# Column halves for the last expert's second weight alone, eight split output rows, and zero products before the last left half

## Chip, cores, metric

One core of one Trainium2 chip. The metric is the device time of one execution in microseconds (us); lower is better. The span of the trace is some 1.8 us shorter than that time. Most of what follows happens in the last 25 us of about 157.

## The reference

Attention with a per-head mask feeds a soft mixture of experts. Only its last part matters here:

```python
for e in range(E):                                   # 8 experts, 4 slots each
    h = np.maximum(slot_input[e] @ w1[e], 0.0)
    slot_out[e] = h @ w2[e]                          # w2[e]: 1024 x 512, float32
slot_out = slot_out.reshape(n_slots, D)
c = softmax(logits, axis=1)                          # 3072 x 32
return (c @ slot_out).astype(np.float32)             # 3072 x 512, 6 MB
```

Every output row needs the slots of all eight experts, so no row is final before the last w2 has landed. A column of the output needs only that column of each w2.

## The kernel before

The weights are loaded from float32 in HBM to bf16 in SBUF by GpSimd's DMA queue, one load after the other; w2 of experts 5, 6 and 7 comes last. It comes in column halves, all left halves first, so that the left columns of some output rows can be computed and stored while the right halves still load. In this document 5L is the left half of expert 5's w2, 7R the right half of expert 7's, and so on. A "row" r is one of 24 groups of 128 output rows (256 KB); a left or right half row has 128 KB.

```python
    def w_half(e, cs):
        nc.gpsimd.dma_start(w2s[e][:, :, cs], w2v[e][:, :, cs])
    # ... (cut)
    w_half(5, left)
    # ... w_half(6, left), w_half(7, left) (cut)
    for e in (5, 6, 7):
        w_half(e, right)
    # ... attention's end, expert products of the first layer, experts 0 to 4 (cut)
    for e in (5, 6, 7):
        second(e, (0,), spread=True)          # 8 products of 256 columns each: left half
    NL = 12                                   # rows that are split
    # product(): one matmul to a PSUM bank, evicted and scaled by DVE (even r) or ACT (odd r)
    V.tensor_copy(slot_out[:, left], sp[0])
    half_rows(left, 0, (2, 2, 4, 4), (1, 2), nc.gpsimd)      # left halves of rows 0 to 11, 4 stores
    for e in (5, 6, 7):
        second(e, (1,), spread=True)          # right half
    V.tensor_copy(slot_out[:, right], sp[1])
    # rows 12 to 23 whole: groups of 1, 1, 2, 4, 4 rows, stored by nc.sync (cut)
    half_rows(right, 2, (4, 4, 4), (1, 2), nc.sync)          # right halves of rows 0 to 11
```

The softmax here doesn't subtract the row's maximum and nothing guards it: scores larger than these inputs give would overflow.

Of the kernel before, what the change touches and what calls it, by code (L numbers as in the profile page):

```python
# [10 lines left out]
F32 = mybir.dt.float32  # L11
# [27 lines left out]
def kernel(  # L39
# [13 lines left out]
    nc = tc.nc  # L53
    P = 128
# [3 lines left out]
    NE, DM, F = moe_w1.shape  # L58
# [16 lines left out]
    def single(shape, dt, name, tag=None):  # L75
        return singles.tile(shape, dt, name=name, tag=tag or name)

    w1s = [single([P, 4, F], BF16, f"w1_{e}") for e in range(NE)]
    w2s = [single([P, 8, DM], BF16, f"w2_{e}") for e in range(NE - 3)] + [None] * 3
# [45 lines left out]
    w2v = [moe_w2[e].rearrange("(fi fo) d -> fi fo d", fo=8) for e in range(NE)]  # L125
# [80 lines left out]
    def x_transpose(n, i0=0, i1=6):  # L206
        b, hp = n // 4, n % 4
        tp = trp.tile([P, S], BF16, tag="tr", name="tpx")
        for i in range(i0, i1):
            nc.tensor.transpose(tp[:, i * 128:(i + 1) * 128], xb[b][:, i, hp * 128:(hp + 1) * 128], ident)  # L210
        nc.vector.tensor_copy(xT[:, hp, i0 * 128:i1 * 128], tp[:, i0 * 128:i1 * 128])  # L211
# [51 lines left out]
    def keep_busy(t, count):  # L263
        for _ in range(count):
            nc.tensor.matmul(t, zero[:, :P], zero, start=True, stop=True)

    idle = pvp.tile([P, 512], F32, tag="pv", name="idle")
# [52 lines left out]
    for n in range(NP):  # L320
# [12 lines left out]
        b, r = n // 4 - 1, n % 4  # L333
# [62 lines left out]
    left, right, full = slice(0, 256), slice(256, 512), slice(0, 512)  # L396

    def w_half(e, cs):
        nc.gpsimd.dma_start(w2s[e][:, :, cs], w2v[e][:, :, cs])  # L399

    w2s[5] = single([P, 8, DM], BF16, "w2_5", tag="msk")
    w_half(5, left)
    w2s[6] = ptp.tile([P, 8, DM], BF16, tag="pT", name="w2_6")
    w_half(6, left)


    def bank(t, shape=(P, 512), dt=F32):
        pool, tag = ((scp, "sc"), (trp, "tr"), (pvp, "pv"))[t]
        return pool.tile(list(shape), dt, tag=tag, name="bank")
# [28 lines left out]
    logits_mm(bl, (0, 1, 2))  # L438
    w2s[7] = ptp.tile([P, 8, DM], BF16, tag="pT", name="w2_7")
    w_half(7, left)  # L440
    for e in (5, 6, 7):
        w_half(e, right)
    x_transpose(last, 0, 3)
    x_transpose(last, 3, 6)
    copies(2, 0)
    idle = bank(2)
# [11 lines left out]
    idle = bank(2)  # L458
# [10 lines left out]
    cs = bank(1, (P, 1))  # L469
# [5 lines left out]
    for e4 in range(2):  # L475
        t = xp.tile([P, 2, 512], BF16, tag="xb", name="hs")
# [29 lines left out]
    idle = spt[1][:, 1]  # L506

    def second(e, xs=(0, 1), spread=False):
        e4, g = e // 4, e % 4
        for fo in range(8):  # L510
            c = fo % 4 if spread else g
            for x in xs:
                nc.tensor.matmul(sp[x][32 * c:32 * c + 32, :], hT[e4][:, fo, 32 * g:32 * g + 32],  # L513
                                 w2s[e][:, fo, 256 * x:256 * x + 256],
                                 start=(e4 == 0 and fo == 0), stop=(e == 7 and fo >= 4))
# [11 lines left out]
    for r in range(24):  # L527
        e = expR.rearrange("c (p r) -> c r p", r=24)[:, r]
        er.append(e)
        nc.tensor.matmul(rp[:, r:r + 1], e[:ES], ones[:ES], start=True, stop=True)  # L530
    V.reciprocal(rrow, rp)
    for e in (5, 6, 7):
        second(e, (0,), spread=True)


    NL = 12
    ov = out.rearrange("(p r) d -> p r d", r=24)

    def product(r, o, cs, t):
        op = bank(t, (P, cs.stop - cs.start))  # L540
        nc.tensor.matmul(op, er[r], slot_out[:, cs], start=True, stop=True)  # L541
        if r % 2:
            nc.scalar.activation(o, op, ACT.Copy, scale=rrow[:, r:r + 1])  # L543
        else:
            V.tensor_scalar(o, op, rrow[:, r:r + 1], None, op0=ALU.mult)  # L545

    def half_rows(cs, t0, groups, banks, eng):
        ots = [single([P, n, 256], F32, f"oh{t0 + x}", tag=f"w1_{t0 + x}") for x, n in enumerate((8, NL - 8))]
        r = 0
        for rows in groups:  # L550
            for _ in range(rows):
                product(r, ots[r // 8][:, r % 8], cs, banks[r % len(banks)])
                r += 1
            eng.dma_start(ov[:, r - rows:r, cs], ots[(r - 1) // 8][:, (r - rows) % 8:(r - 1) % 8 + 1])

    V.tensor_copy(slot_out[:, left], sp[0])  # L556
    half_rows(left, 0, (2, 2, 4, 4), (1, 2), nc.gpsimd)
    for e in (5, 6, 7):
        second(e, (1,), spread=True)
    V.tensor_copy(slot_out[:, right], sp[1])  # L560
    r = NL
    for t, groups in enumerate(((1, 1, 2), (4,), (4,))):
        ot, base = single([P, 4, DM], F32, f"ot{t}", tag=f"w1_{4 + t}"), r
        for rows in groups:
            for _ in range(rows):
                product(r, ot[:, r - base], full, (1, 2)[r % 2])
                r += 1
            nc.sync.dma_start(ov[:, r - rows:r, :], ot[:, r - rows - base:r - base])
    half_rows(right, 2, (4, 4, 4), (1, 2), nc.sync)


# [33 lines left out]
```

## Time and profile before

| kernel before | |
|---|---|
| time, median of 6 runs | 157.33 us (156.19 to 157.59) |
| span of the trace | 155.7 us |
| last load (7R) lands | 137.82 us |
| first full-row store issued | 140.40 us |
| last packet of output ends | 154.04 us |

All rows but the first come from the trace; its clock starts at the first instruction. The prediction below shows the lines. "DMA" is the busy share of the core's 16 DMA engines in tenths and "GB/s" what they moved, in 40 equal slices. PE is the engine of the matrix products (PEld loads its weights), DVE and ACT evict and scale results, and GpSimd (POOL) and SP issue DMAs here. The granted clock of PE is 1.00 at full speed and 0.50 at half; "zero products" below are matmuls of zeros whose only use is to keep PE busy. One more line, from the DMA issues (output and input, queue, count, KB each, median us from issue to landing), serves as a yardstick for stores:

```profile
out_dram<-ot SPq DMA_DIRECT2D x2, 256.0 KB, 2.2
```

These are the first two full-row stores. They land 2.2 us after their issue.

### The profile page before, as it was taken

Reading aid. Unit: us, or ns where it says so; the run is one execution under the profiler, and the core shown is the slowest. Engines: PE = TensorE matmul, PEld = TensorE weight load, DVE = VectorE, ACT = ScalarE, POOL = GpSimd, SP = SyncE. Lnnn points to the kernel's source line nnn. Section 1 sums busy time; section 2 is a strip of 40 time slices with the busy share of each in tenths; the row PEclk is TensorE's granted clock in tenths of the full one; section 3 lists DMA queues with packets and bytes.
Section 4 is the critical chain, followed back from the end, with each engine's and each line's share of the span. In section 5 each row is a group of like instructions: output and inputs, shape, how many; then the busy total and the mean of one; then the engine's idle time right before and its main releaser. Section 6 shows DMA issues by size and latency. Waiting matters only on the chain. (4 is left out here: it accounts for less than half of the span.)

```text
span 155.7 us, 5051 instructions
## 1 busy us (share of the span) xinstructions
PE 118.2 (76%) x2239; PEld 74.6 (48%) x2239; DVE 106.8 (69%) x247; ACT 109.8 (71%) x148; POOL 41.1 (26%) x57
## 2 busy tenths in 40 slices
PE   6756598878697979977979979778987897449500
PEld 2324365555465645755656556555633476214300
DVE  2896269999987869978769979678735414429700
ACT  3286489979799998999898999999451512408700
POOL 7673043720350260170084200000480000700000
PEclk9975559999999999999999999999999999956975
DMA  3999999999999999999999999999999999977995
GB/s 54 155 184 203 172 218 203 196 187 189 212 219 202 188 216 198 186 222 195 186 219 200 185 211 223 213 217 215 210 223 190 199 196 199 240 290 283 404 355 183
DMA packets 40535, 32.85 MB, mean 211 GB/s; under 512 B 26050, under 2 KB 37826, under 8 KB 38594
## 3 DMA queue, kind: packets, MB, share of 16 engines
q0 software_dynamic: 38208, 27.82, 115.1%
q1 hardware_dynamic: 2306, 4.72, 8.1%
q8 instruction: 17, 0.28, 0.7%
q14 instruction: 4, 0.03, 0.1%
HBM read 52.49 MB, written 6.29 MB: 377 GB/s over the span
## 5 line engine op out<-in xcount | busy, mean ns | idle before, releaser
L172 ACT ACTIVATE pT<-sc 128x1024 bf16<-128x1024 f32 (+1 forms) x96 | 83.4, 923 | 9.3 <-PE sc L167 8.8
L167 PE MATMUL sc<-Tq,Tk 64*128 64x256 bf16 (+3 forms) x320 | 36.5, 292 | 13.6 <-ACT Tk L151 10.0
L193 PEld LDWEIGHTS <-pT 128*128 128x128 bf16 x672 | 24.9, 99 | 12.2 <-issue 8.0
L184 DVE TENSOR_TENSOR pT<-pT,msk 128x1024 bf16<-128x1024 bf16 (+1 forms) x48 | 29.3, 639 | 0.2 <-ACT pT L172 0.2
L193 PE MATMUL pv<-vb,pT 128*128 128x65 bf16 x352 | 27.5, 196 | 0.3 <-DVE xb L202 0.3
L193 PE MATMUL pv<-vf,pT 128*128 128x65 bf16 x320 | 25.3, 197 | 0.0
L167 PEld LDWEIGHTS <-Tk 64*128 64x128 bf16 x320 | 11.2, 95 | 22.6 <-ACT Tk L151 13.2
L141 PEld LDWEIGHTS <-raw 64*64 64x64 bf16 x768 | 15.9, 115 | 10.8 <-issue 7.4
L111 POOL DMA_DIRECT2D raw<-in_q_dram x10 | 6.4, 639 | 49.5 <-PE tpk L141 48.3
L148 DVE COPY Tq<-tpq 128x768 bf16<-128x768 bf16 x16 | 15.3, 956 | 4.8 <-PE tpq L141 4.6
L202 DVE TENSOR_TENSOR xb<-pv,rs 128x384 bf16<-128x384 f32 x32 | 17.8, 557 | 1.1
L151 ACT COPY Tk<-tpk 128x768 bf16<-128x768 bf16 x16 | 12.9, 805 | 5.0 <-PE tpk L141 5.0
L201 DVE RECIPROCAL rs<-pv 128x6 f32<-128x6 f32 x32 | 6.2, 193 | 11.9 <-PE pv L193 11.9
L118 POOL DMA_DIRECT2D vb<-in_v_dram x8 | 11.6, 1451 | 1.1 <-issue 0.9
L141 PE MATMUL tpk<-ident,raw 64*64 64x64 bf16 x384 | 9.8, 202 | 2.3 <-DVE Tq L148 1.3
L399 POOL DMA_DIRECT2D w<-in_moe_w_dram x6 | 5.2, 879 | 22.3 <-PE sc L167 20.1
L141 PE MATMUL tpq<-ident,raw 64*64 64x64 bf16 x384 | 9.6, 200 | 1.7 <-DMA raw<-in_q_dram 1.7
L541 PE MATMUL bank<-slot_out,expR 128*128 128x256 bf16 (+1 forms) x36 | 9.2, 368 | 1.9 <-DVE slot_out L556 0.5
L210 PE MATMUL tpx<-ident,xb 128*128 128x128 bf16 x96 | 8.1, 218 | 2.0 <-ACT expT L224 1.1
L211 DVE COPY xT<-tpx 128x768 bf16<-128x768 bf16 (+1 forms) x17 | 9.0, 528 | 0.8 <-PE tpx L210 0.8
L543 ACT ACTIVATE ot<-bank,rrow 128x512 f32<-128x512 f32 x6 | 3.9, 686 | 6.5 <-PE bank L541 6.5
L541 PEld LDWEIGHTS <-expR 128*128 128x128 bf16 x36 | 5.1, 153 | 6.3 <-issue 5.7
(86 smaller groups left out, 117.3 us busy)
## 6 DMA issues: line engine op xcount, KB each, us to landing
w<-in_moe_w_dram POOLq DMA_DIRECT2D x13, 1024.0 KB, 18.3
vb<-in_v_dram POOLq DMA_DIRECT2D x8, 384.0 KB, 13.0
w<-in_moe_w_dram POOLq DMA_DIRECT2D x6, 512.0 KB, 17.8
raw<-in_q_dram POOLq DMA_DIRECT2D x6, 384.0 KB, 10.2
raw<-in_k_dram POOLq DMA_DIRECT2D x6, 384.0 KB, 11.4
out_dram<-ot SPq DMA_DIRECT2D x2, 1024.0 KB, 4.6
out_dram<-oh SPq DMA_DIRECT2D x3, 512.0 KB, 6.3
out_dram<-oh POOLq DMA_DIRECT2D x2, 512.0 KB, 6.8
```

Of the source, the lines that this page charges most:

```text
L118: nc.gpsimd.dma_start(vbs[m % 3].rearrange("p h j d -> p (h j) d")[:, :, :D], v[b, h:h + 4].rearrange("h (j p) d -> p (h j) d", p=P))
L141: nc.tensor.transpose(tp[po, s, :], src[po, 64 * s:64 * s + 64], ident[po, po])
L148: nc.vector.tensor_copy(o, i)
L151: nc.scalar.copy(o, i)
L167: nc.tensor.matmul(sc[:, hh, at:at + 128 * cnt], kT[n][po:po + 64, j * 128:(j + 1) * 128], qT[n][po:po + 64, i0 * 128:(i0 + cnt) * 128], s ...
L172: nc.scalar.activation(pT[n][:, :, o:o + ln], sc[:, :, :ln], ACT.Exp, scale=scale)
L184: nc.vector.tensor_mul(x, x, m)
L193: nc.tensor.matmul(pv[n][:, i % 3, hh, :], pT[n][:, hh, o:o + 128], vv[:, hh, j, :D + 1], start=(j == 0), stop=(j == i))
L202: nc.vector.tensor_mul(xb[b][:, 3 * half:3 * half + 3, h * D:(h + 2) * D].rearrange("p i (h d) -> p i h d", h=2), pv[n][:, :, :, :64], rs. ...
L210: nc.tensor.transpose(tp[:, i * 128:(i + 1) * 128], xb[b][:, i, hp * 128:(hp + 1) * 128], ident)
L211: nc.vector.tensor_copy(xT[:, hp, i0 * 128:i1 * 128], tp[:, i0 * 128:i1 * 128])
L541: nc.tensor.matmul(op, er[r], slot_out[:, cs], start=True, stop=True)
```

## The change

Intent: large loads move faster than column halves, so split only the last w2. Fewer rows need splitting then; PE is kept at full clock through the wait for 7L; the first full row is evicted by two engines at once so that its store leaves earlier.

```diff
-    w_half(5, left)
+    nc.gpsimd.dma_start(w2s[5], w2v[5])
-    w_half(6, left)
+    nc.gpsimd.dma_start(w2s[6], w2v[6])
@@
     w_half(7, left)
-    for e in (5, 6, 7):
-        w_half(e, right)
+    w_half(7, right)
@@
-    for e in (5, 6, 7):
-        second(e, (0,), spread=True)
-    NL = 12
+    second(5, spread=True)
+    second(6, spread=True)
+    keep_busy(idle, 7)                        # 7 zero products of 128x512
+    second(7, (0,), spread=True)
+    NL = 8
@@
-    half_rows(left, 0, (2, 2, 4, 4), (1, 2), nc.gpsimd)
-    for e in (5, 6, 7):
-        second(e, (1,), spread=True)
+    half_rows(left, 0, (2, 2, 4), (1, 2), nc.gpsimd)
+    second(7, (1,), spread=True)
@@
-    for t, groups in enumerate(((1, 1, 2), (4,), (4,))):
+    for z, groups in enumerate(((1, 1, 2), (4,), (4,), (4,))):
@@
-                product(r, ot[:, r - base], full, (1, 2)[r % 2])
+                if r == NL:
+                    for t, cs in ((1, left), (2, right)):
+                        product(r, ot[:, 0, cs], cs, t)
+                else:
+                    product(r, ot[:, r - base], full, (1, 2)[r % 2])
@@
-    half_rows(right, 2, (4, 4, 4), (1, 2), nc.sync)
+    half_rows(right, 2, (4, 4), (1, 2), nc.sync)
```

(Cut: the tiles of the half rows, and the choice of engine by bank instead of by row.)

More of the change, by code (lines that the diff above doesn't have):

```diff
@@ L541, in product @@
         nc.tensor.matmul(op, er[r], slot_out[:, cs], start=True, stop=True)
-        if r % 2:
+        if t == 2:
             nc.scalar.activation(o, op, ACT.Copy, scale=rrow[:, r:r + 1])
@@ L547, in half_rows @@
     def half_rows(cs, t0, groups, banks, eng):
-        ots = [single([P, n, 256], F32, f"oh{t0 + x}", tag=f"w1_{t0 + x}") for x, n in enumerate((8, NL - 8))]
-        r = 0
+        ot, r = single([P, NL, 256], F32, f"oh{t0}", tag=f"w1_{t0}"), 0
         for rows in groups:
             for _ in range(rows):
-                product(r, ots[r // 8][:, r % 8], cs, banks[r % len(banks)])
+                product(r, ot[:, r], cs, banks[r % len(banks)])
                 r += 1
-            eng.dma_start(ov[:, r - rows:r, cs], ots[(r - 1) // 8][:, (r - rows) % 8:(r - 1) % 8 + 1])
+            eng.dma_start(ov[:, r - rows:r, cs], ot[:, r - rows:r])
     V.tensor_copy(slot_out[:, left], sp[0])
-    half_rows(left, 0, (2, 2, 4, 4), (1, 2), nc.gpsimd)
-    for e in (5, 6, 7):
-        second(e, (1,), spread=True)
+    half_rows(left, 0, (2, 2, 4), (1, 2), nc.gpsimd)
+    second(7, (1,), spread=True)
     V.tensor_copy(slot_out[:, right], sp[1])
     r = NL
-    for t, groups in enumerate(((1, 1, 2), (4,), (4,))):
-        ot, base = single([P, 4, DM], F32, f"ot{t}", tag=f"w1_{4 + t}"), r
+    for z, groups in enumerate(((1, 1, 2), (4,), (4,), (4,))):
+        ot, base = single([P, 4, DM], F32, f"ot{z}", tag=f"w1_{4 + z}"), r
         for rows in groups:
             for _ in range(rows):
-                product(r, ot[:, r - base], full, (1, 2)[r % 2])
+                if r == NL:
[3 more added lines that the diff above has]
+                    product(r, ot[:, r - base], full, (1, 2)[r % 2])
                 r += 1
             nc.sync.dma_start(ov[:, r - rows:r, :], ot[:, r - rows - base:r - base])
-    half_rows(right, 2, (4, 4, 4), (1, 2), nc.sync)
+    half_rows(right, 2, (4, 4), (1, 2), nc.sync)
 _INS = ['q', 'k', 'v', 'is_retrieval', 'n_sink', 'window', 'moe_phi', 'moe_w1', 'moe_w2']
```

## The prediction

> **What bounds the kernel now.** I read the chain that ended last first, in order of time, then the stretches table around its longest piece, then the DMA view and the timeline of the end. The chain (start us, us, what):
>
> ```profile
> 113.05 2.59 POOL w L399 x3
> 115.64 22.18 DMA w<-in_moe_w_dram
> 137.82 0.04 issue
> 137.86 0.64 PE bank L513 x8
> 138.50 0.02 issue
> 138.52 0.44 DVE slot_out L560
> 138.96 0.04 issue
> 139.00 3.97 PE bank L541 x9
> ...
> 144.88 2.17 ACT oh L543 x5
> ```
>
> What sets the end is no engine but one load: the right column half of the last w2 (7R below; 5L, 5R and so on likewise), which lands at 137.82. After it come eight expert products, one cast and the output rows. The last row is evicted at 147.05, but the span is 155.7 us: the rest is stores still moving, which the chain does not follow. The stretches table (stretch and length in us; busy of PE, PEld, DVE, ACT, POOL; granted clock; DMA share; GB/s) tells how fast the data moves:
>
> ```profile
> 113.00:117.00 4.00, 3.52 (x34) 1.26 (x25) 1.31 (x4) 2.06 (x5) 3.46 (x4) 1.00 1.03 215
> 125.00:129.00 4.00, 3.73 (x90) 2.88 (x79) 0.42 (x1) 0.58 (x1) 0.00 (x0) 1.00 1.45 197
> 133.00:137.00 4.00, 1.31 (x20) 0.64 (x19) 1.00 (x3) 1.09 (x3) 2.44 (x4) 0.87 1.21 267
> 137.00:141.00 4.00, 2.62 (x13) 1.10 (x13) 1.70 (x3) 0.78 (x2) 0.00 (x0) 0.50 0.61 228
> 145.00:149.00 4.00, 1.37 (x8) 0.77 (x6) 1.94 (x5) 2.04 (x5) 0.00 (x0) 1.00 1.00 399
> 149.00:153.00 4.00, 0.00 (x0) 0.00 (x0) 0.00 (x0) 0.00 (x0) 0.00 (x0) 0.58 1.02 342
> ```
>
> Full w2 loads run at 215 GB/s (first row), the column halves at 197 (second). Full-row stores run at 399 (fifth), half-row stores at 342 (last). Between loads and stores (fourth row) the DMA share falls to 0.61 and the clock to 0.50. The DMA view of 132 to 156 us, in 40 slices of 0.6 us, shows that hole:
>
> ```profile
> DMA  9999999999963115999899999999799999995000
> GB/s 192 194 170 265 220 243 343 357 358 378 382 266 143 68 41 212 382 403 423 348 423 410 382 382 382 423 437 410 283 348 336 343 348 345 343 352 169 0 0 0
> ```
>
> Slices 12 to 16 (138.6 to 141.6) carry 266, 143, 68, 41 and 212 where neighbours carry about 385; the first full-row store is issued only at 140.40. From then on the queue is full: output is DMA-bound to the end.
>
> **What the Trainium skill says.** (1) "DMA: Bandwidth & Descriptors", section "Queues, rings and completion order": a DMA engine consumes its ring in order. The trace agrees: left-half stores, issued from 132.5 to 134.7 on the queue of the loads, land at 138.5 to 141.8, behind 7R. (2) Same page, "Latency and other measured facts": two of the engines are usually slower with descriptors from GpSimd. The trace agrees that engines differ: of the sixteen arrivals on 7R's semaphore the first is at 133.5, the median near 136.0, the last two at 137.7 and 137.8. Quick engines are thus free four microseconds before 7R counts as landed. (3) Same page, "Why small descriptors are slow (HBM only)": a fixed overhead per packet; here 215 against 197 GB/s for packets of 8192 and 512 bytes. (4) "TensorE: Matmul & The Clock Gate", "What's actually happening": a quiet window of some 3.4 us halves the clock. The clock records agree: 0.5 from 135.95 to 142.78, after a PE that was mostly idle from 133.9.
>
> **The change part by part.**
> *Loads.* The semaphore arrivals give when each load landed. Full ones: 107.16, 111.98, 116.84, 121.71, so 4.87 us each. Then halves 5L 124.41, 6L 127.03, 7L 129.69, 5R 132.40, 6R 135.17, 7R 137.82: 16.11 us for six, 2.69 each, or 5.37 for a pair. Two pairs become two full loads: 2 x (5.37 - 4.87) = 1.0 us gained. The queue has a backlog then (w2_5 is issued at 109, with loads landing until 121.7), so issue time does not count. New landings: 5 at 126.6, 6 at 131.4, 7L at 134.1, 7R at 136.8.
>
> *Left half.* It now waits for 134.1 instead of 129.69. From the timeline of before: eight products 0.40, a cast 0.43, first product to first eviction 0.31, gaps about 0.1. First eviction at 135.4. Eight rows on two engines at 0.43 per pair start-to-start (six DVE evictions in 2.57 us) take 1.7, to 137.1. POOL started its first store 1.08 after the first eviction and takes 0.74 each: three stores from 136.5 to 138.7.
>
> *Zero products.* Seven of 128x512 at about 0.215 us each start to start (half of the 0.427 at which products of this size follow each other at clock 0.50): 1.5 us, between w2_6's products (done 132.1) and 7L (134.1). They fit, on the critical path they cost nothing. PE is then busy most of 129.8 to 136, so I expect clock 1.0 when 7R lands.
>
> *From 7R to the first full-row store.* Before: 140.40 - 137.82 = 2.58, at half clock: eight products 0.62, cast 0.43, product to eviction 0.63, DVE eviction of 512 columns 0.75, gaps. After, warm: 0.04 + 0.40 + 0.04 + 0.43 + 0.06, then the left half product, the right half about 0.1 behind it, ACT starting 0.41 after and taking 0.47, then issue 0.02: 1.87. Gain 0.71. First full-row store at 136.8 + 1.87 = 138.7, against 140.40: 1.7 us earlier.
>
> *Output after that.* Sixteen full rows and eight half rows instead of twelve and twelve: one more four-row store, one fewer of four half rows. In before, the two four-row stores of full rows landed 2.61 apart (147.20, 149.81) and those of half rows 1.51 apart (151.39, 152.90). Cost 2.61 - 1.51 = 1.1 us. Eviction does not bind: a pair of full rows (512 KB) takes 0.75 us on DVE, but 1.3 us of DMA.
>
> *Left stores beside it.* 1024 KB instead of 1536 on the loads' queue, but issued from 136.5 rather than 132.5. I expect the slowest engine to finish its left stores near 140.0 (before: 141.4), 0.5 us after data of the full rows starts (138.7 + 0.87, from issue to first packet in before = 139.5). Before, this overlap was 0.1 us. I charge 0.2.
>
> Sum: 1.0 + 0.71 gained, 1.1 + 0.2 lost: 0.4 us shorter, some 0.3% of the span. In bytes: the hole at 138.6 to 141.6 is largely closed, but a new one opens from about 133.5 to 137, where quick engines have no loads left and no left rows yet. The output is merely later in bulk.
>
> **Rivals.** *The hole is just moved, nothing is gained (157.3, or up to 158).* For: the left half starts 4.4 us later while 7R is only 1.0 earlier; before, quick engines filled 133.5 to 138.6 with left stores (slices 4 to 11 rise from 265 to 382). Against: the first full-row store is still 1.7 earlier, and that stretch is what feeds the saturated tail. *The left evictions stand in the way.* They end at 137.1 by my sum and the right cast on DVE is wanted at 137.3; only 0.2 us of slack. A late 6 or a cold PE (zero products 3.0 us instead of 1.5, ending after 7L) would push the right half 0.3 to 0.8 us: 157.3 to 157.8. For it speaks the thinness, against it that the PE was warm until 135.95 in before with less work. *The clock is the point, and a warm PE gives more (155.5).* For: the 0.50 from 137 to 141 and products 0.427 us apart. Against: past the first row the DMA is full, and PE speed pays only once, in the 0.71 above. To reach 155.5 the left stores would also have to cost nothing and the start be fed better. No engine looks able to become the bound.
>
> **Range and chances.** The three times of before are 156.19, 157.29 and 157.38, mean 156.95, so the median sits near the top of its spread. The median less 0.4 gives 156.9, the mean less 0.4 gives 156.55; I take 156.7. Repeats spread by 1.2 us, and my sum has errors of about 0.5 in the load gain and 0.7 in the overlap: 155.5 to 157.8. Two per cent is 3.1 us, more than all the load and clock gains together with the extra store cost left out (1.7), so faster gets 0.03; to lose as much the left half would have to fall wholly into the tail, 0.02; within 2% is 0.95.
>
> **What would show it right or wrong.** Right: the products of 7R start near 136.9 on the timeline; the granted clock is 1.00 there; the first full-row store is issued near 138.7; the DMA row shows a dip between 133 and 137 and almost none at 139 to 141; the last rows still land in a saturated queue, about 0.4 us earlier than 154.4. Wrong: 7R lands at 137.5 or later (full loads not quicker); the right cast waits for DVE evictions or PE; the clock falls anyway; the first store to land takes far more than its 2.1 us because left stores hold the slow engines; or the store tail is longer than by 1.1 us.

## The result, and the profile after

The changed kernel takes 159.03 us, median of 6 runs (158.96 to 160.25), against 157.33: ratio 1.0141, 95% interval 1.0097 to 1.0185. Ratios here and below are the mean time of one kernel's fast runs over that of the other's fast runs of the same rounds, so not quite the ratio of the medians. The change is slower by about 2 us, within 2%, but outside the range of the prediction. The traces show it too: 157.2 against 155.7 us.

The chain that ended last, after (start us, us, what):

```profile
110.00 21.41 DMA w<-in_moe_w_dram
131.41 0.04 issue
131.45 0.63 PE bank L512 x16
132.08 0.16 issue
132.24 2.57 PE bank L265 x6
134.80 0.58 PE bank L512 x8
135.38 0.02 issue
135.41 0.44 DVE slot_out L556
...
136.19 1.72 DVE oh L546 x4
137.91 0.41 DVE slot_out L559
```

The long load in the chain is no longer 7R but expert 6's w2, which lands at 131.41. From there the chain runs through work meant to be beside the path: 2.57 us of zero products (L265), then 7L's products at 134.80, although 7L had landed at 134.06, then the left rows. The right cast (L559) follows the last left eviction directly, at 137.91. The landing of 7R is not in the chain at all.

The stretches table (columns as in the prediction):

```profile
133.00:137.00 4.00, 3.22 (x19) 1.36 (x18) 1.24 (x3) 0.70 (x2) 0.00 (x0) 0.64 0.47 63
137.00:141.00 4.00, 3.59 (x21) 1.79 (x20) 3.53 (x8) 3.27 (x8) 2.19 (x3) 1.00 0.52 178
145.00:149.00 4.00, 0.22 (x2) 0.00 (x0) 0.63 (x2) 0.73 (x2) 0.00 (x0) 1.00 1.03 414
```

From 133 to 137 the DMA engines move 63 GB/s; before it was 267. From 137 to 141 it is 178 against 228. The DMA view from 132 to 157.2 us (slices of 0.63 us here):

```profile
DMA  9977521000669799999999999999999989999000
GB/s 190 153 107 99 77 37 22 0 0 0 221 234 358 241 348 351 335 377 429 397 455 416 416 416 403 416 403 416 416 429 416 416 273 348 346 345 341 24 0 0
```

The hole of before (138.6 to 141.6) is gone, but a larger one has opened: the rate falls from 132.6 on, and from 136.4, when the last packet of the loads ends, to 138.56, the first packet of output, nothing moves at all. Before, the left rows ran here. The first full-row stores, which took 2.2 us to land, now share the engines with left rows, which move until 142.73:

```profile
out_dram<-ot SPq DMA_DIRECT2D x2, 256.0 KB, 4.2
```

**The account.** Counted in the trace's packets, 6144 KB of output leave the core (24 rows of 256 KB). Before, 928 KB of them had started by the time 7R landed; after, none.

| | 7R lands | output moved by then | last packet ends | from 7R to last packet |
|---|---|---|---|---|
| before | 137.82 us | 928 KB | 154.04 us | 16.22 us |
| after | 136.71 us | 0 KB | 155.52 us | 18.81 us |

The loads end 1.11 us earlier. The stretch behind them is 2.59 us longer; at the 327 KB per us that it runs (6144 KB in 18.81 us), 928 KB more are 2.8 us. The difference, 2.59 - 1.11 = 1.48 us, is that of the spans. Summed over its packets, the output takes 16.8 us of the time of all 16 engines before and 16.6 after. So the packets got no slower on the whole; what was lost is time in which the engines had none of them.

### The profile page after: what moved, and what is told of

Same layout as the page of the kernel before. It is cut to its first block, busy times and chain, and to the rows that moved or that the text cites. A ratio compares the mean times of both kernels' runs of the same rounds, so it can differ in the third digit from the quotient of the medians.

```text
span 157.2 us, 5051 instructions
## 1 busy us (share of the span) xinstructions
PE 119.3 (76%) x2241; PEld 74.8 (48%) x2243; DVE 105.8 (67%) x245; ACT 109.5 (70%) x147; POOL 38.0 (24%) x54
## 5 line engine op out<-in xcount | busy, mean ns | idle before, releaser
L544 ACT ACTIVATE oh<-bank,rrow 128x256 f32<-128x256 f32 x8 | 3.5, 474 | 8.7 <-PE bank L542 8.6
L542 PE MATMUL bank<-slot_out,expR 128*128 128x256 bf16 (+1 forms) x33 | 7.9, 323 | 1.7 <-DVE slot_out L556 0.5
L132 POOL DMA_DIRECT2D w<-in_moe_w_dram x12 | 6.6, 556 | 4.3 <-DMA raw<-in_q_dram 2.6
L554 POOL DMA_DIRECT2D out_dram<-oh x3 | 2.2, 737 | 22.4 <-ACT oh L544 22.4
```

Source lines behind the costliest of these rows:

```text
L542: nc.tensor.matmul(op, er[r], slot_out[:, cs], start=True, stop=True)
```

## The experiments

The theory after the result (A): the left rows come too late to use DMA engines that have finished their loads, and their bytes fall into the saturated end. Rivals: (B) the split of the rows, with more full rows behind 7R, is the cost; (C) the zero products at half clock are the cost.

| run | what | ratio to before | 95% interval | 7R lands | moved by then | from 7R to last packet |
|---|---|---|---|---|---|---|
| e1 | before, loads of the change only | 1.0127 | 1.0079 to 1.0174 | 136.52 | 0 KB | 19.06 us |
| e2 | before, split of rows only | 1.0068 | 1.0015 to 1.0122 | 137.35 | 716 KB | 17.15 us |
| e3 | change without zero products | 1.0073 | 1.0031 to 1.0114 | 136.40 | 0 KB | 18.30 us |
| e4 | change, left rows early (wrong result) | 0.9972 | 0.9927 to 1.0017 | 137.01 | 308 KB | 16.76 us |
| e5 | before, PE kept busy | 0.9980 | 0.9934 to 1.0025 | | | |
| e6 | only expert 5 whole | 0.9988 | 0.9951 to 1.0025 | 137.85 | 456 KB | 16.03 us |
| e7 | change without the halved row | 1.0103 | 1.0058 to 1.0149 | 137.89 | 0 KB | 18.02 us |
| e8 | before, 16 left rows | 0.9976 | 0.9934 to 1.0018 | 137.29 | 588 KB | 15.76 us |
| e9 | before, left rows delayed | 1.0122 | 1.0069 to 1.0176 | 136.95 | 0 KB | 20.23 us |
| e10 | change without zeros and halved row | 1.0075 | 1.0042 to 1.0107 | 137.20 | 0 KB | 18.35 us |
| e11 | expert 5 whole, 16 left rows | 0.9992 | 0.9963 to 1.0021 | 136.89 | 444 KB | 16.85 us |
| e12 | e3 with left stores issued by SP | 0.9993 | 0.9963 to 1.0023 | 138.09 | 0 KB | 17.16 us |

The last three columns are of one profiled run each. When the loads end differs by over a microsecond between runs of the same loads (136.40 to 138.09 with two whole loads), so the stretch behind 7R compares better than the span. Medians went from 157.03 us (e4) to 160.59 us (e9). One run each of e2, e5 and e6 and two of e9 count as slow and are left out of the ratios.

### e1: the loads alone

```diff
 # on the kernel before
-    w_half(5, left)
+    nc.gpsimd.dma_start(w2s[5], w2v[5])
-    w_half(6, left)
+    nc.gpsimd.dma_start(w2s[6], w2v[6])
-    for e in (5, 6, 7):
-        w_half(e, right)
+    w_half(7, right)
 # and second(5), second(6) whole before 7's left half; NL stays 12
```

> The kernel before with the loads of the changed kernel alone: w2 of experts 5 and 6 whole, only expert 7's in column halves; 12 left and 12 right half rows, no zero products, no halved row. Theory A (left rows come so late that the DMA queue runs dry and their 1.5 MB fall into the saturated end): slower by 1.2 to 2.2 us, ratio 1.008 to 1.014, although the last load lands 1.1 us earlier, near 136.7; no left-row data before 136.5. Rival B (the split of the rows, with more full rows after the last load, is the cost): not slower, about 1 us faster, because the loads end earlier. Rival C (zero products at half clock are the cost): not slower, as there are none.

1.0127, inside what theory A expected. Neither the split nor zero products are in this kernel, so the load order is enough to lose as much as the whole change does. It ends its loads early (136.52) and has moved no output by then.

### e2: the split alone

```diff
 # on the kernel before
-    NL = 12
+    NL = 8
-    half_rows(left, 0, (2, 2, 4, 4), (1, 2), nc.gpsimd)
+    half_rows(left, 0, (2, 2, 4), (1, 2), nc.gpsimd)
 # one more group of 4 full rows, one group of 4 right half rows fewer
```

> The kernel before with the split of the rows alone: 8 left rows, 16 full, 8 right; loads all in column halves in the old order. Theory A: left stores start at 133 as before but are 0.5 MB less, so the hole between 138.6 and 141.6 widens and that 0.5 MB is paid at the end: slower by 0.8 to 1.3 us, ratio 1.005 to 1.008. Rival B: this is the whole loss, slower by 1.5 to 2.2 us, ratio 1.010 to 1.014. Rival C: no change.

1.0068, as theory A expected and about half of what rival B needs, though the interval reaches into B's range (1.010 or more). With the old loads, fewer left rows cost time; that there is less to fill the engines with fits the 716 KB that had moved when 7R landed, against 928. The effects do not add: e1 and e2 together would be 2% and the whole change is 1.4%. The loads-only kernel with 8 left rows (e10) is at 1.0075 and with 12 (e1) at 1.0127. That fits left rows that hurt when they come late, but the intervals overlap, so a gain of the split in the new order is not shown.

### e3: no zero products

```diff
 # on the changed kernel
-    keep_busy(idle, 7)
```

> The changed kernel without the seven zero products. They took 2.57 us at half clock and held up expert 7's left products by 0.7 us. Theory A: left rows come 0.6 us earlier, the end gains 0.3 to 0.7 us (ratio to before 1.006 to 1.012); not more, as left data still starts only near 138. Rival C: the whole loss is gone, ratio 1.000 or less. If the clock then stays at 0.5 past the last load, the first full-row store is issued up to 0.7 us later and the gain may vanish.

1.0073: part of the loss may go, but not all of it, so rival C is not the whole. The stretch behind 7R is half a microsecond shorter, 18.30 against 18.81 us. The two intervals overlap (1.0031 to 1.0114 and 1.0097 to 1.0185), so the size is uncertain. The mechanism is in the traces: in the stretches table of the changed kernel and then of this one, the window before the clock fell:

```profile
129.01:132.43 3.41, 2.26 (x46) 1.78 (x47) 0.31 (x1) 0.00 (x0) 0.00 (x0) 1.00 1.35 192
```

```profile
128.50:131.90 3.40, 2.08 (x45) 1.66 (x45) 0.31 (x1) 0.00 (x0) 0.00 (x0) 1.00 1.27 186
```

At the end of each the clock went to 0.5, though PE was busy 2.26 of 3.41 us (66%) and 2.08 of 3.40 (61%). The busy share alone does not tell when this happens: in e9 below PE was busy for 3.15 of the 3.42 us before the clock fell at 130.60. In the changed kernel the slow time lasted 3.4 us (to 135.84), in e3 6.8 us (to 138.7). So the zero products cut it by half, but ran in it themselves and held up 7L's products by 0.7 us.

### e4: the left rows early, with a wrong result

```diff
 # on the changed kernel
-    keep_busy(idle, 7)
-    second(7, (0,), spread=True)             # expert 7 is left out of the left half
     V.tensor_copy(slot_out[:, left], sp[0])
     half_rows(left, 0, (2, 2, 4), (1, 2), nc.gpsimd)
+    keep_busy(idle, 7)
     second(7, (1,), spread=True)
 # and the accumulation of the left half is closed at expert 6
```

> The changed kernel, with a wrong result on purpose: expert 7's products are left out of the left half, so the left rows start when w2 of expert 6 has landed (131.4) instead of expert 7's left half (134.1); the seven zero products stand behind the left rows instead of before them. Loads, bytes, row split and halved row are those of the changed kernel. Theory A: left stores are issued from 134 to 136.2 and move on engines that have finished loading; most are done by 139; the end is 1.5 to 2.3 us earlier than the changed kernel, ratio to before 0.994 to 1.000. Rival B (more full rows after the last load, longer tail): still slower than before by over 1 us, ratio 1.008 or more.

0.9972, against 1.0141 of the changed kernel with the same loads, bytes, split and halved row. It stays clear of e3 as well (1.0073, no overlap), which also has no zero products in front of the left rows. The DMA view of 132 to 156 us:

```profile
DMA  9999867797991199999999999999998999990000
GB/s 224 147 129 121 113 87 210 241 369 232 362 328 55 75 382 382 430 403 498 423 369 410 423 382 410 437 423 355 410 423 362 338 345 345 350 338 26 0 0 0
```

The left stores, issued from 134.62, bring the rate back from slice 7 on (135.6) instead of slice 11 there (138.3). More full rows behind 7R are there unchanged, so they are not the loss that is seen; a cost as in e2 (0.7%) may still be in it, paid for by the quicker loads. This is the strongest evidence for theory A: without the later start of the left rows the loss is gone. What it takes away is the wait for 7L, so this is no version to use.

### e9: the left rows late, on the kernel before

```diff
 # on the kernel before
+    keep_busy(idle, 20)
     V.tensor_copy(slot_out[:, left], sp[0])
     half_rows(left, 0, (2, 2, 4, 4), (1, 2), nc.gpsimd)
```

> The kernel before with 20 zero products on PE in front of the left rows, and nothing else: at full clock 4.3 us, so the left rows start near 135 instead of 131 and their stores are issued from about 136, as in the changed kernel; loads, split and bytes as before. Theory A (the lateness of the left rows is the cost): slower by 0.8 to 1.7 us, ratio 1.005 to 1.011. Rival B (row split or loads, not lateness): ratio 1.000. Rival D (the engine that finishes its loads last sets the end; it has left rows waiting for it at 137.8 either way): ratio 1.000 to 1.003.

1.0122, a little over the expected range, with loads and split as before. (The two runs left out, 161.38 and 162.01 us, had clocks like the others; with them the loss would be larger.) The DMA view of 132 to 156 us has the hole of the changed kernel:

```profile
DMA  9999884100005797999999999999999998999999
GB/s 185 193 183 157 117 115 63 23 0 0 0 0 191 246 335 225 307 328 355 328 338 365 382 437 403 457 423 396 396 396 437 382 410 331 318 353 335 352 345 343
```

The delay was larger than planned: again the clock was at 0.5 for part of the zero products (130.6 to 134.0), they took 5.92 us, and the left stores were issued at 138.23. PE then had the left rows before it at 7R's landing, so the first full-row store also came late, at 141.80. The run shows what lateness costs, not lateness of the left rows alone; e4 covers that side. Rival D of its expectation (an engine that is last with its loads has left rows waiting either way) does not hold here, though the late full rows have a part in that.

### e12: the left stores on SP's queue

```diff
 # on e3
-    half_rows(left, 0, (2, 2, 4), (1, 2), nc.gpsimd)
+    half_rows(left, 0, (2, 2, 4), (1, 2), nc.sync)
```

> The changed kernel without zero products, with its left stores issued by SP instead of GpSimd. A store there is issued in 0.33 us instead of 0.74 and its first packet came 0.87 us after the issue started instead of 1.29. Left rows alone moved at 270 to 340 GB/s on the GpSimd queue. Theory A: the empty stretch ends about 0.4 us sooner and left rows move faster: 0.4 to 1.0 us earlier than without zero products, ratio 1.001 to 1.005. Rival (only the time at which the rows are evicted counts): same as without zero products, 1.007.

0.9993, better than theory A expected: with no other edit than this, e3's loss of 0.7% is gone (the intervals do not overlap). The DMA view of e3 and then of e12, 132 to 156 us:

```profile
GB/s 192 173 148 123 108 40 17 0 0 177 259 328 219 341 369 328 376 417 396 492 423 396 396 410 423 382 410 410 410 410 410 423 311 348 346 350 343 186 0 0
```

```profile
GB/s 180 155 120 102 99 72 35 13 12 8 0 265 353 328 345 350 381 376 417 410 492 410 437 355 423 437 410 369 437 410 369 410 437 294 350 352 340 348 188 0
```

In e3 the rate climbs by way of 177, 259, 328, 219; in e12 it is at 265 and 353 within two slices. From the issue of the first left store to its first packet it is 0.92 us in e12 and 1.29 in e3; from that issue to the last packet of all, 17.48 and 18.26 us. So lateness alone is not the loss. No output had moved here either when 7R landed, and the first left store was issued 2.30 us after 7L's landing, in e3 2.68; yet nothing is lost. By this run the loss belongs to late left rows on GpSimd's queue, where output starts again slowly once the engines have run dry. Of the 0.78 us between the two stretches, 0.37 is the wait for the first packet; the rest lies behind it, and not in slower packets: the output takes 16.6 and 16.7 us of the engines' time (e3, e12). Whether SP's queue would help the kernel before too, whose left stores wait behind loads, was not tried; if it did, not all of this gain would be the refilling. The profiled run of e12 was the slowest of its six, with 7R 1.7 us later than in e3, which is why its span (156.8) says little.

### e7 and e10: the halved first row

```diff
 # on the changed kernel (e7); e10 also without keep_busy(idle, 7)
-                if r == NL:
-                    for t, cs in ((1, left), (2, right)):
-                        product(r, ot[:, 0, cs], cs, t)
-                else:
-                    product(r, ot[:, r - base], full, (1, 2)[r % 2])
+                product(r, ot[:, r - base], full, (1, 2)[r % 2])
```

> The changed kernel with its first full row evicted whole by DVE, as before. At full clock a whole row takes 0.75 us on DVE against 0.48 for the two halves beside each other: first full-row store 0.2 to 0.3 us later. Theory A: at that time the left rows hold the queue (they move until 142.7), so the end does not change: within 0.3 us of the changed kernel, ratio to before 1.012 to 1.016. Rival (first store to end one to one): 0.3 us slower than the changed kernel.

> The changed kernel without zero products and without the halved row: whole loads of 5 and 6 and the split of 8 rows. Against the loads-only kernel (1.0127 with 12 left rows) it shows what the split is worth when the left rows come late; against the kernel without zero products (1.0073) what the halved row is worth. Theory A: late left rows delay 7R and hold the queue, so fewer of them are better here: 1.006 to 1.009; the halved row is worth 0.3 us at most.

e7 is at 1.0103, below its expected range and below the changed kernel (1.0141), with overlapping intervals; e10 at 1.0075 is level with e3 at 1.0073, which has the halved row. No worth of the halved row shows. The profiled run of e7 was one in which the clock never fell near the end: the zero products took 1.46 us (x6) instead of 2.57, and the first left store came 2.41 us after 7L's landing instead of 3.21. That run was no faster for it (159.37 us), which again speaks against rival C. Its clock too was at 0.5 in mid-kernel (43.2 to 50.0), and its loads landed some 1.2 us later than in the changed kernel. So the clock during the zero products differs from run to run, although the code up to there is the same.

### e8: more left rows, e6 and e11: one whole load

```diff
 # e8, on the kernel before
-    NL = 12
+    NL = 16
-    half_rows(left, 0, (2, 2, 4, 4), (1, 2), nc.gpsimd)
+    half_rows(left, 0, (2, 2, 4, 4, 4), (1, 2), nc.gpsimd)
 # one group of 4 full rows fewer, one of 4 right half rows more
```

```diff
 # e6, on the kernel before; e11 is e6 with the 16 left rows of e8
-    w_half(5, left)
+    nc.gpsimd.dma_start(w2s[5], w2v[5])
-    for e in (5, 6, 7):
+    for e in (6, 7):
         w_half(e, right)
 # and second(5) whole
```

> The kernel before with 16 left rows, 8 full ones and 16 right ones: the opposite of the changed split, loads as before. The hole of 138.6 to 141.6 gets 0.5 MB more to carry. Theory A without regard to engines: 0.8 to 1.1 us faster, ratio 0.993 to 0.995. With the slowest engine as the bound: it is busy from 137.8 without a gap either way and the further half rows cost 0.2 us more in small packets, so within 0.4 us, ratio 0.998 to 1.002.

> The kernel before with w2 of expert 5 alone whole; 6 and 7 stay in column halves, left halves first. By the measured landings 7L comes at 132.0 (2.3 later than before) and 7R at 137.3 (0.5 earlier). Left rows are issued from about 134.9. Theory A: these are ready before the slow engines have finished loading, but 2.4 us later than before, so the quick engines lose some of their filling: between -0.5 and +0.5 us, ratio 0.997 to 1.003. Rival (the loss is one for one with the lateness of the left rows): half of the 2.0 us of the loads-only kernel, ratio 1.006.

> A version meant to beat both: w2 of expert 5 whole, 6 and 7 in column halves, and 16 left rows. Sixteen left rows filled the hole completely in the kernel before (span 154.7); the whole load ends the loads 0.5 us earlier and brings the left rows 2.3 us later. Theory A: 0.3 to 1.2 us faster than before, ratio 0.992 to 0.998. If lateness counts one for one, not faster than 1.000.

None of the three is clear of the kernel before: 0.9976, 0.9988 and 0.9992, each interval with 1 in it. The DMA view of e8, 132 to 156 us, is what a full queue looks like:

```profile
DMA  9999999999999999999999999999999999600000
GB/s 191 193 192 187 235 196 315 329 345 389 382 362 328 362 348 352 382 396 413 437 417 423 410 355 341 326 364 340 340 343 353 350 341 348 227 0 0 0 0 0
```

No hole is left, and the profiled span is 154.7 us, but over six runs the gain is only 0.2% and may be nothing. What it saves in the hole it partly pays in right half rows, the slices at about 345 at the end where full rows have 410. e8 misses what theory A expected without regard to engines (0.993 to 0.995), though its interval covers it. e6 shows that 2.5 us later left rows (issued at 134.96) can be borne when they still start before 7R has landed: 456 KB were moved by then. Its interval (to 1.0025) leaves out the rival by which lateness costs one for one (1.006). e11 was meant to beat both kernels; it beats the changed one but not the one before, and lies outside its expected range of 0.992 to 0.998.

### e5: PE kept busy in the kernel before

```diff
 # on the kernel before
-    for e in (5, 6, 7):
-        second(e, (1,), spread=True)
+    for e, z in ((5, 0), (6, 4), (7, 7)):
+        keep_busy(idle, z)
+        second(e, (1,), spread=True)
```

> The kernel before with zero products in the two PE waits after the left rows: four before 6R, seven before 7R, so that the clock is 1.00 when 7R lands. Theory A with the engines in mind (the engine that finishes the loads last carries its share of left rows until 141.4 in the kernel before, so an earlier first full-row store helps only the quick ones): first full-row store 0.4 to 0.6 us earlier, near 139.9, end 0 to 0.5 us earlier, ratio 0.997 to 1.000. Rival (the way from the last load to the first store sets the end one to one): ratio 0.996 or less. If the zero products run at half clock they hold up 7R and it is slower.

0.998 with an interval of 0.9934 to 1.0025: no gain shown. One of its six runs, the profiled one, was slow, with the clock at 0.5 for a while in mid-kernel, so its trace is not used and whether its first store came earlier stays open.

## Why the prediction was wrong

- **The bound and the loads: right.** I gave 126.6, 131.4, 134.1 and 136.8 for the landings; they were 126.58, 131.41, 134.06 and 136.71. In this pair of traces the whole loads are quicker by the 1.0 us of the sum. That it fits so well is in part luck: from the landing of expert 4's w2 to that of 7R it took 16.10 us before and 15.05 after, but up to 16.19 (e12) in other runs with the same two whole loads.
- **"They fit, on the critical path they cost nothing" (zero products): wrong.** I took 0.215 us each at full clock. The clock was at 0.5 from 132.43 to 135.84 and they took 2.57 us instead of 1.5. That is the rival "left evictions stand in the way", which I named and put aside because PE had stayed warm in before. Why the clock fell here at 132.43 and in before only at 135.95 stays open. The left rows ended near 138.0 instead of 137.1, 7R's products had to wait until 137.43, and the first full-row store was issued at 139.24 instead of 138.7: 0.5 us. The way from 7R's products to that store took 1.81 us, as in the sum (1.87 with the 0.04 before them). That the clock was at 1.00 for 7R's products was right.
- **"Left stores beside it ... I charge 0.2": the step that failed most.** When the first full-row store was issued, 1500 of 1536 KB of left rows had started in before and 244 of 1024 KB after. I reckoned with an end of the left rows near 140.0; their last packet ended at 142.73. From the first full-row store to the last packet it took 13.64 us before and 16.28 after; my terms were 1.1 for the full rows and 0.2 for the overlap. The 1.1 held (four-row stores of full rows landed 2.6 and 2.5 apart, those of right half rows 1.5), so the overlap was 1.5. I had seen the new hole from 133.5 to 137 and wrote that the output is "merely later in bulk", but gave the bytes missing there no term. The first left store was issued 0.8 us later than I had it, and its first packet came 1.29 us after that.
- **The sum.** 0.5 and 1.3 us too little: -0.4 became +1.4 by these terms, +1.5 on the traces.
- **The rivals.** "The hole is just moved" was the right one, and e4 and e9 show it from both sides; its size was too low, as I let it cost only what the rest gained. By e12 the hole costs this much only with the left stores on GpSimd's queue. "The clock is the point" has no support: nothing that kept PE warm gained.
- **Open.** How the loss divides between zero products and late left rows is known only roughly, as the intervals of e3 and of the changed kernel overlap; the worth of the halved row and of the split in the new order is within noise. What left stores on SP's queue would do in the kernel before is not known.

## What to carry to other kernels

When the end of a kernel is a saturated store queue, count the bytes that have left by the time the last input lands; an earlier last load can be worth nothing if it empties the queue of output that used to run beside it. The bytes alone do not decide: ask also how fast the output starts again, as e12 had moved none by then and lost nothing. Cheaper loads bought by making the first partial result wait can lose more than they gain, and a hole in the DMA row must be given a price in bytes, not just a place. Filler work put in front of a wait must fit at half clock too.

## What the Trainium skill lacked or had wrong

- "TensorE: Matmul & The Clock Gate", table of the two states: the clock is said to fall after an idle window of about 3.4 us. Here it fell at the end of stretches of 3.4 us in which PE was busy for 50% (before, at 135.95, where the prediction saw agreement), 66% (changed kernel, at 132.43) and 92% (e9, at 130.60), with matmul ends modelled; and it stayed at 1.00 after one with 62% (changed kernel, 142.67 to 146.08). So an idle window is not needed, and the busy share alone does not tell when it falls; the page gives no such share.
- "DMA: Bandwidth & Descriptors", section "Latency and other measured facts", says that two of the engines are usually slower. In the changed kernel 7R's sixteen arrivals were at 133.0 to 134.0 for eight and at 135.0 to 136.7 for the other eight: half of the engines were behind by one microsecond or more, three by over two.
- Same page: first bytes after about 1 us from GpSimd and 0.6 from SP. From the start of the issue to the first packet it was 1.29 and 0.92 us here (e3, e12). The page has nothing on how an empty queue fills: the first slices of left stores moved 177 and 259 GB/s from GpSimd and 265 and 353 from SP.
